# Softmax factors made beside an expert's second layer, from a copy of their logits

## The chip, the core and the metric

The kernel runs on one core of a Trainium2 chip. The metric is device time in microseconds (us) of one execution, as the median of several. A core has a matrix engine (PE, whose weight loads are listed as PEld), a vector engine (DVE), an activation engine (ACT), GpSimd (POOL) and a queue engine (SP) that here issues most of the DMAs. Each engine runs its own instructions strictly in their order, and an instruction that waits holds up all that stand behind it.

## What is computed

A recurrent attention is followed by a mixture of eight experts and a second pair of layers. The part that matters here is the mixture:

```python
logits = x @ w_gate
e_idx = np.argmax(logits, axis=1)
probs = np.exp(logits - logits.max(-1, keepdims=True))
probs /= probs.sum(-1, keepdims=True) + 1e-09
gate_w = probs[np.arange(N), e_idx]
eom = 1.0 / (1.0 + np.exp(-(x @ w_output_gate)))
for e in range(E):
    mask = e_idx == e
    h = np.maximum(x[mask] @ w1[e], 0.0)
    out[mask] = gate_w[mask, None] * eom[mask, e, None] * (h @ w2[e])
```

Then comes `relu(out @ w_in)**2 @ w_out`. The factor `gate_w * eom` of a row is not needed before the very last layer: there its square multiplies the row of the result. It is called the factor below.

## The kernel before

The program has three parts one after the other: the attention with the routing of the rows (about 560 us), the eight experts (about 270 us) and the second pair of layers (about 370 us). The change lies in the part of the experts.

**An expert** (e0 to e7) has 448 rows in a dense pass. Its first layer makes eight blocks of hidden values, f0 to f7, each with eight matmuls into a PSUM tile `ph` (line 1185). There are three such tiles, so block f4 can only start when block f1 has been read out of its tile. It is read by ACT (`hw`, line 1253, the high part) and then by DVE (`hw`, line 1254, the low part); both read `ph`. After blocks f5, f6 and f7 the PE also makes four transposes each (line 1226) for the next expert's rows `x`. The second layer is 64 matmuls (line 1356) in three groups: 16, 24 and 24. A group ends with a read by ACT (`yT`) and a DMA to `yTD` on SP (line 1365).

**The weights** of the next expert come in pieces (the generator `pieces`): SP loads a piece into one of four slots of `raws` (line 909), ACT makes its rounded high part (line 922) and POOL subtracts to get the low part (line 923), which frees the slot for the next load. The ACT instruction for a piece stands after each of the blocks f0 to f5, and there are two more in the second layer.

**Beside the second layer** the function `beside(e, s, nxt)` is called with s = 0, 1, 2, 3, before the matmuls 0, 16, 32 and 48. With s = 0 it loads the rows of the expert after next (`load_x`, line 1237). With s = 0, 1 and 2 it makes a step of `wide`, which turns a block of 64-bit weights into 32-bit ones: an ACT instruction (line 1151), five on DVE (lines 1152 to 1155 and 1167), one on POOL (line 1156) and a load of a later block on SP (line 1141). With s = 3 it issues the first four loads of the weights of the expert after next on SP.

**The factors** come from `gates`, a generator of three steps that is run in the first layer, one step after each of the blocks f0, f1 and f2. The first step has two small DVE instructions (lines 987 and 988), the second two on ACT (exponentials, lines 990 and 991), and the third six on DVE (lines 993 to 999) on tiles of 128 x 4 values, one of which reads 128 x 32. After the last block, ahead of the second layer, two DMAs on SP (line 1342) write the tile `gt` to `gtD` in DRAM, at a place that is only known at run time. Both write the same DRAM tensor at such places, and SP waits for the first to land before it issues the second. At the turn to the second pair SP loads all of `gtD` into `GT` (line 1383), and a DVE instruction `TID` (line 1384) reads it ahead of the pair's other DVE work.

All instructions of this part stand in an order written out by hand, which is the order of the code, engine by engine. At its very end, around the turn to the second pair, some of them are interleaved with those of the next part.

Of the kernel before, what the change touches and what calls it, by code (L numbers as in the profile page):

```python
# [7 lines left out]
F32 = mybir.dt.float32  # L8
# [4 lines left out]
AF = mybir.ActivationFunctionType  # L13
# [5 lines left out]
B, H, S, D = 4, 8, 768, 40  # L19
T = 32  # tokens of a chunk  # L20
NCH = S // T
WIN = 12  # chunks between two rescalings of the state
W_LO, W_HI = 0.84, 1.13  # decays that the scaled form covers
RSC = 2.0**24  # centres W_LO^(T WIN) .. W_HI^(T WIN) in the range of the square root
E = 8
ARENA = 12288  # words of a partition: the weights of an expert in two parts
F1 = 1024
F2 = 2048
CAP = 448  # rows of an expert that the dense pass covers
RS = 3200  # rows reserved per expert  # L30
NOV = 24  # blocks of 128 rows beyond CAP, at most
NP = 104  # partitions of the (head of pair at 0 / 64, feature) layout
# [5 lines left out]
XW = 402  # a routed row: 320 values, the last 64 again, 16 logits, number of the token (twice)  # L38
Y0 = 128  # the first of the tokens by expert, without gaps
YR = Y0 + S * B + CAP  # with room for the padding of the last expert  # L40
# [30 lines left out]
def layout(r, k, v, w, a, b, moe_w_gate, moe_w_output_gate, moe_w1, moe_w2, moe2_w_in, moe2_w_out):  # L71
# [7 lines left out]
    def tr(x):  # chunk, head of pair, feature, (pair, batch), token  # L79
        return x.reshape(B, 4, 2, NCH, T, D).transpose(3, 2, 5, 1, 0, 4).reshape(NCH, 2, D, 16, T)  # L80

# [13 lines left out]
    def rows(z):  # 320 rows as 128 + 128 + 64 twice  # L95
        z = np.concatenate([z, z[..., 256:320, :]], axis=-2)
        z = z.reshape(z.shape[:-2] + (3, 128, z.shape[-1]))
        return np.moveaxis(z, -3, -2)
# [14 lines left out]
ORDER = [  # stage, chunk relative to the iteration, argument  # L113
# [38 lines left out]
TAIL = [  # the last two iterations: stage, chunk relative to the last one, argument  # L152
# [73 lines left out]
HEAD = [  # the stages before the first regular iteration: stage, chunk, argument  # L226
# [70 lines left out]
EARLY = [2, 3, 5, 0]  # the first chunks for which DVE does a share of GpSimd's work  # L297


def attention(ctx, tc, nc, A, K, R, nch=NCH, order=ORDER, head=HEAD, tail=TAIL):  # L300
# [20 lines left out]
    def early(shape):  # L321
        """part of the arena: the buffers here are done with some chunks before the end"""
# [74 lines left out]
    # ---- loads  # L397
# [33 lines left out]
    # ---- decays: W (before a token) and C (after it), scaled a, b, k  # L431
# [20 lines left out]
    def A_rec2(c):  # L452
        # third-order step: 1 / C = y (t^2 - 3 t + 3), t = C y
# [27 lines left out]
    # ---- a.b and a.k of all pairs of tokens of a chunk  # L481
# [56 lines left out]
    # ---- inverse of the unit triangular system: 16 x 16 blocks, then the pair  # L538
# [65 lines left out]
    # ---- state  # L604
# [82 lines left out]
    # ---- outputs  # L687
# [72 lines left out]
    # ---- routing  # L760
# [49 lines left out]
def program(tc, A, out, nch=NCH, order=ORDER):  # L810
    nc = tc.nc
    V, G, S_, P = nc.vector, nc.gpsimd, nc.scalar, nc.tensor
    with ExitStack() as top:
# [31 lines left out]
        # ---- routing of 128 tokens  # L845
# [28 lines left out]
        def beyond():  # L874
            """whether there are rows beyond CAP, or decays out of range, or too few of the rows that are read ahead"""
# [22 lines left out]
        W1E = [732 * i for i in range(7)] + [5120, 5632]  # pieces of an expert's weights, the last 64 columns of the second ones apart  # L898
        W2I = [768 * i for i in range(9)]

        def pieces(slot, src, at, slots=4):
            """weights as the sum of two float32r parts, piece by piece"""
# [11 lines left out]
            for i in range(len(at) - 1):  # L914
                rw = ahead.pop(i)
                if at[i + 1] == 5632:  # high and low parts side by side
# [17 lines left out]
        def first_piece():  # L934
            if not first_w:
                first_w.extend([pieces(0, A["we"][0], W1E, 3)])
            elif not ring:  # in the place of the arena
                ring.append(cp.tile([128, ARENA], F32, name="ring0", tag="arena"))
            drain(first_w[0], 1)

        def zero(k):
            """rows of zeros: no row of xsD is read before it is written"""
# [8 lines left out]
        def rows_ahead():  # L951
            """rows that expert 0 most likely has already, without its last chunks"""
# [6 lines left out]
        def flag(pm):  # L959
            """whether a decay was out of range"""  # L960
# [19 lines left out]
        def gates(pool, x, g, e):  # L980
            """g: token (0) and the square of its factor (1) for the rows x (logits in 384:400) of expert e, step by step;
            relu(g a)^2 = g^2 relu(a)^2 as g >= 0"""
            a8 = list(x.shape[:-1]) + [8]
            L, O = x[..., 384:392], x[..., 392 + e]
# [8 lines left out]
            V.tensor_copy(g[..., 0], x[..., 400])  # L993
# [7 lines left out]
        def places():  # L1001
            """where the rows of an expert start in ysD"""
# [3 lines left out]
        def blocks(pool):  # L1006
            """the last blocks of 128 rows of an expert, beyond CAP"""
            V.tensor_scalar(out=pv, in0=pv, scalar1=0.0, scalar2=None, op0=ALU.max)
            # the first 512 rows are read before the dense pass of the last expert: if it has a part of them,
            # all its rows count as beyond CAP, and come before those of the other experts  # L1010
# [20 lines left out]
        with ExitStack() as ctx:  # L1031
# [5 lines left out]
            with tc.If(other > 0):  # L1037

                # ---- general path for decays out of range: token by token
# [40 lines left out]
                # ---- rows beyond CAP  # L1080
                blocks(op)
                for e in [E - 1] + list(range(E - 1)):
# [3 lines left out]
                    with tc.For_i(0, n_e, 1) as i:  # L1086
# [7 lines left out]
                        drain(gates(op, xo, go, e))  # L1094
# [31 lines left out]
        # ---- expert layers  # L1126
# [6 lines left out]
        def widths(src, n, step, ready):  # L1133
            """float64 weights, as pairs of words, to float32 (rounded to nearest), step by step"""
# [8 lines left out]
            def front(o):  # L1143
                """c: bits of |w|, the high word's 20 of the mantissa, then plus the low word's rounded"""
# [27 lines left out]
        def split_x(pk, x3, k, c):  # L1172
            """x3: [128, 5, n]: hi0 lo0 hi1 lo1 (hi2; lo2)"""
# [34 lines left out]
        def load_y(i):  # L1208
            """512 columns of the second layer pair's input, in the order of the experts"""
# [18 lines left out]
        with ExitStack() as ctx:  # L1228
# [22 lines left out]
            def hidden(ph, t, c):  # L1251
                """columns c of the hidden values: high parts, low parts"""
# [219 lines left out]
```

## Time and profile before

| | |
|---|---|
| Time, median of three executions | 1192.63 us (1191.32 to 1192.74) |
| Profiled execution: its time from first to last instruction (span) | 1201.3 us |
| of which attention and routing, experts, second pair | 560, 270.4, 370.9 us |
| Busy in the span: PE, PEld, DVE, ACT, POOL | 86%, 76%, 69%, 54%, 40% |
| Granted clock of PE over the span | 0.876 of full speed |

The profile comes from one execution that was recorded, and it is 8.7 us longer than the median of those that were only timed. No time other than the span is given for it. Stretches and durations are read from it; a difference of two stretches is carried over to the median as it is.

### The profile page before, as it was taken

Reading aid. Unit: us, or ns where it says so; the run is one execution under the profiler, and the core shown is the slowest. Engines: PE = TensorE matmul, PEld = TensorE weight load, DVE = VectorE, ACT = ScalarE, POOL = GpSimd, SP = SyncE. Lnnn points to the kernel's source line nnn. Section 1 sums busy time; section 2 is a strip of 40 time slices with the busy share of each in tenths; the row PEclk is TensorE's granted clock in tenths of the full one; section 3 lists DMA queues with packets and bytes.
Section 4 is the critical chain, followed back from the end, with each engine's and each line's share of the span. In section 5 each row is a group of like instructions: output and inputs, shape, how many; then the busy total and the mean of one; then the engine's idle time right before and its main releaser. Section 6 shows DMA issues by size and latency. Waiting matters only on the chain.

```text
span 1201.3 us, 31764 instructions
## 1 busy us (share of the span) xinstructions
PE 1038.2 (86%) x13114; PEld 911.5 (76%) x13114; DVE 829.3 (69%) x1827; ACT 652.6 (54%) x1407; POOL 476.9 (40%) x465
## 2 busy tenths in 40 slices
PE   2688888888897778887988889998989999999997
PEld 2577777777786666767877778886879998998986
DVE  6999998989989999653675566536993434344442
ACT  6587786776686776672444434334443343443432
POOL 6556464554554645341455455435541010101011
PEclk9977785869576886787989899999999999999999
DMA  5843333333332332243576667535330000000000
GB/s 139 265 124 83 87 93 86 98 83 92 86 92 72 104 86 70 82 122 125 133 200 168 179 188 187 146 115 131 104 97 23 27 23 27 23 1 23 2 21 22
DMA packets 56236, 114.99 MB, mean 96 GB/s; under 512 B 14608, under 2 KB 30096, under 8 KB 54160
## 3 DMA queue, kind: packets, MB, share of 16 engines
q1 hardware_dynamic: 50656, 100.47, 30.9%
q0 software_dynamic: 2688, 8.88, 1.9%
q10 hardware_dynamic: 2736, 3.49, 0.9%
q8 instruction: 106, 1.74, 0.6%
q14 instruction: 50, 0.41, 0.1%
HBM read 89.39 MB, written 23.43 MB: 94 GB/s over the span
## 4 chain that ended last, share of the span: by engine, by line
PE 31%; DVE 12%; DMA 6%; ACT 2%; issue 1%; SPq 1%; POOL 0%; POOLq 0%; ACTq 0%; DVEq 0%
PE ph L1185 17%; PE po L1189 4%; PE po L1190 4%; PE po L1188 4%; DMA raws<-in_we_dram 2%; PE py L1356 2%; DMA q<-in_wi_dram 2%; DVE c L1153 1%; DVE hl L1408 1%; DVE q L1405 1%; DVE c L1167 1%; DVE gm L996 1%; DVE gt L997 1%; DVE gt L999 1%; DVE c L1154 1%
## 5 line engine op out<-in xcount | busy, mean ns | idle before, releaser
L1185 PE MATMUL ph<-x,ring 128*128 128x512 f32 (+2 forms) x1344 | 319.7, 387 | 27.2 <-DVE hw L1254 27.2
L1185 PEld LDWEIGHTS ph<-x,ring 128*128 128x128 f32 x1344 | 249.5, 197 | 63.0 <-DVE hw L1254 30.0
L923 POOL TENSOR_TENSOR ring<-raws,ring 128x732 fp32r<-128x732 f32 (+2 forms) x72 | 124.1, 1744 | 137.2 <-ACT ring L922 108.3
L1405 DVE TENSOR_TENSOR q<-r 128x512 f32<-128x512 f32 x96 | 73.0, 761 | 106.8 <-ACT r L1404 106.8
L1423 POOL DMA_INDIRECT out_dram<-o,TID x24 | 28.2, 1175 | 269.6 <-ACT o L1421 226.7
L1189 PE MATMUL po<-ring,hl 128*128 128x320 f32 x368 | 115.6, 314 | 7.3 <-DVE hl L1408 7.3
L1188 PE MATMUL po<-ring,hh 128*128 128x320 f32 x368 | 114.6, 311 | 2.8 <-ACT hh L1407 2.8
L474 POOL TENSOR_TENSOR arena<-arena 40x1024 f32<-40x1024 f32 x43 | 108.5, 2523 | 20.2 <-ACT arena L456 16.0
L1404 ACT ACTIVATE r<-ph 128x512 f32<-128x512 f32 x96 | 57.1, 595 | 108.6 <-PE ph L1185 108.6
L1190 PE MATMUL po<-ring,hh 128*128 128x320 f32 x368 | 114.2, 310 | 0.0
L1408 DVE TENSOR_TENSOR hl<-q,hh 128x512 fp32r<-128x512 f32 x92 | 72.5, 788 | 54.8 <-ACT hh L1407 54.8
L1407 ACT ACTIVATE hh<-q 128x512 fp32r<-128x512 f32 x92 | 58.2, 633 | 88.0 <-DVE q L1405 88.0
L1356 PE MATMUL py<-hw,ring 128*128 128x448 f32 x512 | 105.4, 365 | 0.0
L1356 PEld LDWEIGHTS py<-hw,ring 128*128 128x128 f32 x512 | 95.5, 188 | 7.6
L1254 DVE SCALAR_TENSOR_TENSOR hw<-ph,hw 128x448 fp32r<-128x448 f32 (+2 forms) x72 | 39.7, 567 | 88.2 <-ACT hw L1253 88.1
L1189 PEld LDWEIGHTS po<-ring,hl 128*128 128x128 f32 x368 | 69.6, 189 | 14.9 <-DVE hl L1408 11.1
L1188 PEld LDWEIGHTS po<-ring,hh 128*128 128x128 f32 x368 | 69.8, 190 | 7.5 <-ACT hh L1407 3.2
L450 POOL TENSOR_TENSOR arena<-Cx,arena 104x512 f32<-104x512 f32 x22 | 26.3, 1197 | 123.6 <-ACT xs L862 115.7
L1190 PEld LDWEIGHTS po<-ring,hh 128*128 128x128 f32 x368 | 69.7, 189 | 0.0
L922 ACT ACTIVATE ring<-raws 128x732 fp32r<-128x732 f32 (+2 forms) x72 | 56.9, 792 | 22.8 <-DMA raws<-in_we_dram 20.5
L1253 ACT ACTIVATE hw<-ph 128x448 fp32r<-128x448 f32 (+2 forms) x72 | 35.8, 498 | 57.8 <-PE ph L1185 57.6
L439 DVE TENSOR_TENSOR_SCAN Cx<-arena 104x528 f32<-104x528 f32 x24 | 61.0, 2540 | 7.0 <-DMA arena<-in_xE_dram 6.3
(215 smaller groups left out, 2257.7 us busy)
## 6 DMA issues: line engine op xcount, KB each, us to landing
raws<-in_we_dram SPq DMA_DIRECT2D x48, 366.0 KB
arena<-in_xE_dram SPq DMA_DIRECT2D x48, 322.5 KB
xL<-in_xL_dram SPq DMA_DIRECT2D x24, 480.0 KB
xsD<-raws SPq DMA_DIRECT2D x24, 268.0 KB
q<-in_wi_dram SPq DMA_DIRECT2D x16, 384.0 KB
xg<-xsD SPq DMA_DIRECT2D x7, 804.0 KB
q<-in_wo_dram SPq DMA_DIRECT2D x16, 320.0 KB
wb<-in_wB_dram SPq DMA_DIRECT2D x24, 165.0 KB
```

The source lines that it names most:

```text
L439: V.tensor_tensor_scan(out=Cx.rearrange("p a b->p (a b)"), data0=s["w"], data1=d1[0:NP].rearrange("p a b->p (a b)"), initial=0.0, op0=ALU. ...
L474: (V if c < EARLY[2 + hh] else G).tensor_tensor(out=bd[sl, :, :, hh].rearrange("p a b c x->p (a b) c x"), in0=s["bk"][sl].rearrange("p (a ...
L923: G.tensor_tensor(out=lo, in0=rw, in1=hi.bitcast(F32), op=ALU.subtract)
L1185: P.matmul(ps, t[:, o : o + 128], x3[:, i, c], start=(j == 0), stop=(j == 7))
L1188: P.matmul(ps, hh, whi[:, o : o + 320], start=start, stop=False)
L1189: P.matmul(ps, hl, whi[:, o : o + 320], start=False, stop=False)
L1190: P.matmul(ps, hh, wlo[:, o : o + 320], start=False, stop=stop)
L1356: P.matmul(py, w, x, start=(f == 0 and k == 0), stop=last)
L1404: S_.activation(r, ph, AF.Relu)
L1405: V.tensor_tensor(out=q, in0=r, in1=r, op=ALU.mult)
L1407: S_.activation(hh, q, AF.Copy)
L1408: V.tensor_tensor(out=hl, in0=q, in1=hh.bitcast(F32), op=ALU.subtract)
```

## The change

`gates` is no longer drained in the first layer. At the start of an expert's first layer one ACT instruction copies the 18 columns of the logits and the token number of each row into a new tile `gl` (line 1333 of the new kernel). A new generator `factors` runs `gates` on that copy and ends with the two DMAs to `gtD` (line 1307 of the new kernel). `beside` runs one step of it with s = 0, 1 and 2, ahead of its other work. `gates` now takes columns 0 to 17 instead of 384 to 401; the rare path for rows beyond the dense pass passes it the columns accordingly. Comments were also taken out.

```diff
-            L, O = x[..., 384:392], x[..., 392 + e]
+            L, O = x[..., 0:8], x[..., 8 + e]
...
-            V.tensor_copy(g[..., 0], x[..., 400])
+            V.tensor_copy(g[..., 0], x[..., 16])
...
-                def beside(e, s, nxt):
+                def factors(e, off):
+
+                    gt = ep.tile([128, 4, 2], F32, name="gt", bufs=2)
+                    gl = glog.pop(e)
+                    yield from gates(ep, gl, gt, e)
+                    why = "the experts have at most S * B rows together"
+                    for j, n in ((0, 384), (3, 64)):
+                        p = min(n, 128)
+                        at = nc.s_assert_within(off + 128 * j, 0, YR - n, skip_runtime_bounds_check_because=why)
+                        nc.sync.dma_start(out=gtD[bass.ds(at, n)].rearrange("(j p) x->p j x", p=p), in_=gt[0:p, j : j + n // p])
+
+                def beside(e, s, nxt, gate):
+                    if s < 3:
+                        drain(gate, 1)
                     if s < 2 + (e == 0):
                         drain(nxt[2], 1)
...
-                    gt = ep.tile([128, 4, 2], F32, name="gt", bufs=2)
-                    gate = gates(ep, xg[e], gt, e)
+                    gl = glog[e] = ep.tile([128, 4, 18], F32, name="gl", bufs=2)
+                    S_.activation(gl, xg[e][:, :, 384:XW], AF.Copy)
...
-                        drain(gate, 1)
...
+                    gate = factors(e, off)
                     why = "the experts have at most S * B rows together"
-                    for j, n in ((0, 384), (3, 64)):
-                        p = min(n, 128)
-                        at = nc.s_assert_within(off + 128 * j, 0, YR - n, skip_runtime_bounds_check_because=why)
-                        nc.sync.dma_start(out=gtD[bass.ds(at, n)].rearrange("(j p) x->p j x", p=p), in_=gt[0:p, j : j + n // p])
...
-                            beside(e, i // 16, nxt)
+                            beside(e, i // 16, nxt, gate)
```

On DVE, this is the first layer of e3 in the kernel before: the low parts `hw` of the blocks, and between those of the third and the fourth block the six instructions of the last step of `gates`.

```order
L1254 SCALAR_TENSOR_TENSOR hw<-ph,hw 128x448
L987 TENSOR_REDUCE gm<-xg 128x4
L988 TENSOR_TENSOR gd<-xg,gm 128x32
L1254 SCALAR_TENSOR_TENSOR hw<-ph,hw 128x448 x2
L993 COPY gt<-xg 128x4
L995 TENSOR_REDUCE gm<-gd 128x4
L996 TENSOR_SCALAR gm<-gm 128x4
L997 SCALAR_TENSOR_TENSOR gt<-gt,gm 128x4
L998 RECIPROCAL gt<-gt 128x4
L999 TENSOR_TENSOR gt<-gt 128x4
L1254 SCALAR_TENSOR_TENSOR hw<-ph,hw 128x448 x3
```

After the change the last three groups of DVE in the second layer of e2 are these: the six instructions of e2's factors, a step of `wide` (`c` and `q` are its tiles), and then e3's first layer.

```order
L993 COPY gt<-gl 128x4
L995 TENSOR_REDUCE gm<-gd 128x4
L996 TENSOR_SCALAR gm<-gm 128x4
L997 SCALAR_TENSOR_TENSOR gt<-gt,gm 128x4
L998 RECIPROCAL gt<-gt 128x4
L999 TENSOR_TENSOR gt<-gt 128x4
L1152 TENSOR_SCALAR c_13003<-q_12938 128x384
L1153 TENSOR_SCALAR c_13003<-c_13003 128x384
L1154 TENSOR_SCALAR c_13003<-c_13003 128x384
L1155 TENSOR_SCALAR c_13003<-c_13003 128x384
L1167 SCALAR_TENSOR_TENSOR c_12966<-q_12728,c_12966 128x384
L1254 SCALAR_TENSOR_TENSOR hw<-ph,hw 128x448 x6
```

So six low parts of e3 now follow each other with nothing between them, and the six small instructions stand ahead of the step of `wide` with s = 2.

On SP, this is what stands in the second layer of e2 before: the end of the two DMAs to `gtD`, the rows of e4, the loads `q` of `wide`, two results `yTD`, and the first four weight loads for e4.

```order
L1342 DMA gtD<-gt 64x2
L1237 DMA xg<-xsD 128x4x402
L1141 DMA q_12942<-in_wi_dram 128x768
L1365 ISA
L1365 DMA yTD<-yT 64x448
L1141 DMA q_12977<-in_wi_dram 128x768
L1141 DMA q_13006<-in_wi_dram 128x768
L1365 REGISTER_ALU
L1365 DMA yTD<-yT 128x448
L909 DMA raws<-in_we_dram 128x732 x4
```

And this is the same place after the change.

```order
L1237 DMA xg<-xsD 128x4x402
L1141 DMA q_12938<-in_wi_dram 128x768
L1375 ISA
L1375 DMA yTD<-yT 64x448
L1141 DMA q_12975<-in_wi_dram 128x768
L1307 ISA
L1307 DMA gtD<-gt 128x3x2
L1307 ISA
L1307 DMA gtD<-gt 64x2
L1141 DMA q_13012<-in_wi_dram 128x768
L1375 REGISTER_ALU
L1375 DMA yTD<-yT 128x448
```

The row that follows is again that of the four weight loads. The two DMAs to `gtD` now stand between the second and the third load `q`, so the third `q`, a result and the four weight loads queue behind them.

## Rows read from the trace of the kernel before

**Rows 1.** Busy time per stretch: the first layers of e1 to e7.

```profile
core 0: us, PE busy (x) PEld busy (x) DVE busy (x) ACT busy (x) POOL busy (x), PEclk, DMA share, GB/s
596.74:619.54 22.80, 18.30 (x78) 15.60 (x76) 15.07 (x24) 10.38 (x20) 12.69 (x8) 0.85 0.66 194
632.46:653.70 21.24, 16.87 (x77) 14.32 (x75) 11.01 (x17) 9.95 (x19) 10.32 (x6) 0.92 0.64 175
666.85:689.50 22.65, 18.06 (x77) 15.31 (x76) 11.71 (x17) 9.96 (x19) 10.30 (x6) 0.85 0.63 168
702.42:724.40 21.98, 17.58 (x77) 14.82 (x75) 11.54 (x17) 10.07 (x19) 10.29 (x6) 0.84 0.67 171
737.57:758.08 20.51, 17.51 (x78) 15.16 (x76) 11.74 (x17) 10.30 (x19) 10.33 (x6) 0.83 0.64 152
771.00:789.71 18.71, 16.73 (x78) 14.40 (x76) 10.97 (x17) 10.13 (x19) 10.35 (x6) 0.91 0.45 135
802.85:817.63 14.78, 13.07 (x65) 11.92 (x64) 9.57 (x16) 9.90 (x18) 10.12 (x6) 1.00 0.74 250
```

**Rows 2.** The same view for the second layer of e2.

```profile
653.70:666.85 13.15, 13.15 (x66) 12.13 (x66) 10.32 (x18) 4.51 (x9) 6.94 (x5) 1.00 0.67 180
```

**Rows 3.** Timeline of DVE, first layers of e0 and e3: start, us, instruction.

```profile
576.62 0.16 DVE L997 SCALAR_TENSOR_TENSOR gt<-gt,gm 128x4 f32<-128x4 f32 x1
...
675.04 1.29 DVE L993 COPY gt<-xg 128x4 f32<-128x4 f32 x1
...
678.08 1.65 DVE L997 SCALAR_TENSOR_TENSOR gt<-gt,gm 128x4 f32<-128x4 f32 x1
...
681.36 1.67 DVE L1254 SCALAR_TENSOR_TENSOR hw<-ph,hw 128x448 fp32r<-128x448 f32 x3
```

**Rows 4.** Timeline of PE, first layers of e0 and e3; idle time in brackets.

```profile
578.77 1.89 PE L1185 MATMUL ph<-x,ring 128*128 128x256 f32 x8 [2.68 <-DVE hw L1254]
...
673.82 3.49 PE L1185 MATMUL ph<-x,ring 128*128 128x448 f32 x16 [0.41 <-DVE hw L1254]
677.15 0.69 PE L1226 MATMUL pk<-cst,xg 128*128 128x128 f32 x4
682.02 3.36 PE L1185 MATMUL ph<-x,ring 128*128 128x448 f32 x8 [4.18 <-DVE hw L1254]
```

**Rows 5.** Timeline of SP, first to sixth expert.

```profile
598.71 1.98 SPq L909 DMA_DIRECT2D raws<-in_we_dram  x4
...
662.43 3.06 SPq L1141 DMA_DIRECT2D q<-in_wi_dram  x2
...
666.19 2.27 SPq L909 DMA_DIRECT2D raws<-in_we_dram  x4
...
681.46 3.92 SPq L1342 DMA_DIRECT2D gtD<-gt  x2
...
735.13 1.85 SPq L909 DMA_DIRECT2D raws<-in_we_dram  x4
...
767.50 1.82 SPq L909 DMA_DIRECT2D raws<-in_we_dram  x4
```

**Rows 6.** Waits of SP, experts: line, waited for, us in total, times, longest.

```profile
SPq L1342 <- DMA gtD<-gt: 25.7, 8, 4.6
```

**Rows 7.** Timeline of DVE and POOL in the second layer of e2.

```profile
655.56 1.82 DVE L1153 TENSOR_SCALAR c<-c 128x384 f32<-128x384 f32 x1
...
661.80 0.55 DVE L1167 SCALAR_TENSOR_TENSOR c<-q,c 128x384 int32<-128x384 int32 x1
...
662.03 1.20 POOL L1156 TENSOR_TENSOR c<-c,r 128x384 int32<-128x384 int32 x1 [1.15 <-DVE c L1155]
...
664.55 0.55 DVE L1167 SCALAR_TENSOR_TENSOR c<-q,c 128x384 int32<-128x384 int32 x1
669.23 0.62 DVE L1254 SCALAR_TENSOR_TENSOR hw<-ph,hw 128x448 fp32r<-128x448 f32 x1 [4.12 <-ACT hw L1253]
```

**Rows 8.** The chain that ended last, around the second layer of e2.

```profile
666.19 5.66 DMA raws<-in_we_dram
671.87 0.82 ACT ring L922
```

**Rows 9.** Granted clock after an idle PE in e1's first layer.

```profile
605.20:610.10 4.90, 4.86 (x16) 4.35 (x17) 4.12 (x5) 3.35 (x9) 4.90 (x4) 0.65 0.88 270
```

**Rows 10.** Timeline at the turn to the second pair.

```profile
832.98 0.43 SPq L1383 DMA_DIRECT2D GT<-gtD  x1
...
837.50 0.18 DVE L1384 CAST TID<-GT 128x24 int32<-128x24 f32 x1 [4.93 <-DMA GT<-gtD]
```

More of the change, by code (lines that the diff above doesn't have):

```diff
@@ L1093, in program @@
                         go = op.tile([128, 1, 2], F32, name="go")
-                        drain(gates(op, xo, go, e))
+                        drain(gates(op, xo[..., 384:XW], go, e))
                         nc.sync.dma_start(out=w1t.rearrange("p a b->p (a b)"), in_=A["we"][e, :, 0 : 3 * F1])
@@ L1311, in beside @@
                         drain(wide, 1)
+                glog = {}
                 wide = work()
```

## The prediction

> **What bounds the kernel now.** I read the stretches first, then the timelines of PE, DVE and SP over two experts, then the waits and the chain. The change lies in the 270 us of the experts. Their second layers need no help: e2's takes 13.15 us for 64 matmuls, PE is busy throughout and the granted clock is 1.00 [rows 2]. That is 0.205 us for a matmul.
>
> The first layers of e1 to e6 have the same 64 matmuls and three groups of four transposes, 0.69 us each [rows 4], a little less where they overlap. At the same rate that is 13.1 + 1.9 = 15.0 us, but they take 18.71 to 22.80 us [rows 1]. e7 has no transposes: 14.78 us against 13.1. So the excess is 7.8, 6.2, 7.6, 7.0, 5.5 and 3.7 us for e1 to e6 and 1.7 us for e7. e0 adds the 2.7 us that its PE sat idle [rows 4]. The sum is **42.2 us**.
>
> In e3 the excess has two causes. The large one comes after block f5: PE sits idle for 4.18 us until a DVE `hw` frees a tile `ph` [rows 4]. DVE began its group of six small factor instructions at 675.04 and only came back to `hw` at 681.36 [rows 3]. Six instructions on four values per partition took 6.3 us. The same instruction, line 997, took 0.16 us in e0 and 1.65 us in e3 [rows 3], where POOL worked without a pause: six instructions, 10.30 us busy in e3's first layer [rows 1]. So most of the six instructions wait for the end of a POOL instruction. The second part is the clock: the eight matmuls after that pause took 3.36 us instead of 1.64 [rows 4], which is the lower level of 1.2 GHz.
>
> The smaller cause is a pause of 0.41 us before f4 [rows 4]. It ends the chain from the weight loads: issued at 666.19, landed 5.66 us later, then an ACT piece ahead of the `hw` of f1 [rows 8]. PE could start f4 at 673.82, 7.6 us after that issue. This second chain is just behind the first layer's own pace, and it is what the change touches with its other hand.
>
> **What is removed.** All eight experts lose the six instructions between the `hw` of their first layer, two small ones before, and two on ACT. I take it that without them the whole excess of 42.2 us would be open to be saved, except what the weight loads hold back. A copy of 128 x 72 values is added on ACT, at the start of the first layer where ACT waits for PE anyway. It is smaller than any ACT instruction on a weight piece, 0.82 us [rows 8]; I take nothing, and at most 8 x 0.8 = 6 us if nothing hid it.
>
> **What is moved on DVE.** In e2's second layer DVE is busy for 10.32 of 13.15 us [rows 2] and stands still from 665.1 to 669.23 [rows 7], so two or three more us there delay no `hw`. Without that gap they would cost 2 us an expert. But POOL works in this layer too, and the small instructions wait for it again: line 1153 took 1.82 us there [rows 7]. The two of the first step stand ahead of that one and take over most of its wait; I add 0.6 us. The six then follow the `wide` instruction that ends at 661.80 + 0.55 = 662.35, or 8.65 us after the layer's start. A POOL instruction runs from 662.03 to 663.23 just then [rows 7]. Lower bound for the six: 6 x 0.16 = 1.0 us; upper bound: 6.3 us as in the first layer [rows 3]. With one POOL instruction in the way I take 2.0 us. So the factors are ready 8.65 + 0.6 + 2.0 = 11.3 us after the layer's start.
>
> **What is moved on SP.** This is where the price is. Before, the two DMAs to `gtD` stood at the end of the first layer, where SP had nothing urgent. The second waits for the first to land: 25.7 us over eight experts, 3.2 us each and at most 4.6 [rows 6]. With both issues the pair takes 3.92 us in e3 [rows 5] and, from the mean wait and two issues of half a us, about 4.3 us on average. After the change, queued behind the pair are a load for `wide`, a result, and the four weight loads, which take part in the second chain above.
>
> Before, these loads were issued 666.19 - 653.70 = 12.5 us after e2's second layer began [rows 1, 5], and e1 and e3 are alike. After: 11.3 + 4.3 + 0.8 for the two issues ahead of them = 16.4 us, so **3.9 us later**. f4 can start 7.6 us after that, at 24.0 us. PE gets there at 13.15 + 6.6 = 19.7 us. The pause before f4 is then 24.0 - 19.7 = 4.3 us. The clock also falls again after such a pause: in e1 PE now pauses in that very place and the 16 matmuls behind it ran at a granted 0.65, 4.86 us instead of 3.3 [rows 9]. I add 1.7 us for each pause over 2 us.
>
> The Trainium skill speaks to the pair: its page "DMA: Bandwidth & Descriptors", section "Anatomy of one DMA", puts a fixed cost of about 2.0 us on a small DMA, most of it the confirmation that the write has landed. The trace differs, with 3.2 us [rows 6], and the trace's number is the one in the sum. With 2.0 us the pause would be 1.2 us shorter in five experts, and the saving 6 us larger.
>
> **The sum.** First layers after the change, excess over 15.0 us: e1 to e4 4 x (4.3 + 1.7) = 24.0 us. I treat e1 like the others: its loads were issued at 598.71 [rows 5], late already, but its `wide` loads will no longer stand behind the pair of e0. e5: its loads were issued 10.7 us after the layer's start [rows 1, 5] and go to 16.0, as one issue less is ahead of them: pause 3.9, with the clock 5.6 us. e6: 9.4 us before [rows 1, 5]; no `wide` load is left there and the factors are ready some 2.5 us earlier, so 13.6, and a pause of 1.5 us. e7 and e0: nothing. Together 24.0 + 5.6 + 1.5 = 31.1 us. Saved: 42.2 - 31.1 = 11.1 us.
>
> At the turn, `GT` is now loaded behind e7's pair and has to wait until its second DMA has landed. Before it was issued at 832.98, 15.4 us after e7's second layer began, and `TID` held DVE until 837.50 [rows 1, 10]. After: e7's factors wait for POOL and for a step of the 64-bit weights between them, so I put the pair at 12 us and its end at 17 or 18. I take off **2 us** (bounds 0 and 5). That leaves **9 us**, and 1192.6 - 9 = 1183.6, given as 1183.
>
> **The rivals.**
> *The loads are not late enough to matter.* If the factors are ready at 10 us and the pair takes 3.2 us, the loads are 1.5 us late and most pauses stay under 2 us with no loss of clock. Then excess stays about 2 us in each of e1 to e5 and some 30 us are saved: 1163 us. For it: DVE is not full in the second layer [rows 2], and the six could slip into a gap with no POOL instruction beside them. Against it: the wait of 3.2 us is a mean over eight [rows 6], and a POOL instruction does run where the six begin [rows 7].
> *Slower: the pair takes longer in its new place.* A `wide` load is issued right ahead of it, and another and the rows of the expert after next shortly before. If the pair lands only behind these, each exposed layer loses the difference. Five are exposed, so 9 us are gone at 1.8 us more, a pair of 6.1 us; at 8 us it would be 1192.6 + 9.5 = 1202. Against it: the pair stood right behind weight loads before, too, and its longest wait was 4.6 us [rows 6].
> On the Trainium skill's page "DMA: Bandwidth & Descriptors", section "Queues, rings and completion order", a completion signal lands only after all earlier writes of its DMA engine, which would be this mechanism; no row here shows whether it is at work.
> *No change:* the pause moves from f6 to f4 and is as long there, 1192 us. The excess after and before would be equal; this is the forecast with 2 us more of wait per expert.
>
> **How the numbers follow.** A measurement of this kernel can tell some 0.2%, 2.4 us, from no change. Forecast (2.4 to 20 us saved): 0.50. Loads hardly late: 0.20. No change: 0.12. Slower: 0.18. So faster 0.70. The range must reach to the gain of the first rival, 1163, and to the slower one near its break-even, 1195: the pair at 6.5 us, or the turn at its upper bound with the pair at 6. About one in ten lies beyond each end.
>
> **What the new profile would show.** Right: no small DVE instruction between the `hw` of a first layer, and the pause of PE gone from f6. `gtD` issued near 11 us into the second layer, weight loads near 16, and a pause of some 4 us before f4 at half the clock behind it. Wrong: weight loads still near 12.5 us (the large gain), or a pair of over 6 us (slower), or a `TID` that comes much later than 20 us after e7's second layer began.

## The result and the profile after

The change makes the kernel **slower**: 1211.24 us, median of four executions (1201.04 to 1213.08), against 1191.97 us (1191.28 to 1192.74) of the kernel before. The ratio is 1.0148, with a 95% interval of 1.0102 to 1.0195. Ratios, here and below, leave out executions more than 1.5% above the fastest of the same kernel and are not the quotients of the medians beside them; the two differ by up to 0.35%. The prediction said 1183 us, with 0.18 for slower.

The profiled execution has a span of 1210.5 us, a granted clock of 0.867 over it and 1212.32 us in the times. Busy shares are PE 87%, PEld 76%, DVE 66%, ACT 54%, POOL 39%. Since single executions of one kernel differ by some 10 us, both kernels were run again later, unchanged. In the stretch from the first matmul of e0 to the first matmul `po` of the second pair the two traces of each give this (starts and ends from the timeline of PE and the windows):

| us | before | before, again | after | after, again | forecast of the change | measured, means |
|---|---|---|---|---|---|---|
| e0 | 36.2 | 36.3 | 32.4 | 32.1 | -2.7 | -4.0 |
| e1 to e6 | 206.1 | 198.8 | 207.2 | 210.1 | -6.7 | +6.2 |
| e7 | 27.6 | 27.6 | 36.2 | 33.3 | -1.7 | +7.1 |
| the turn, up to `po` | 8.6 | 6.8 | 11.6 | 11.8 | +2 | +4.0 |
| sum | 278.5 | 269.5 | 287.3 | 287.3 | -9.1 | +13.3 |

Ahead of e0 and behind `po` the traces of the two kernels show no loss (behind `po` 362.3 us before and 362.0 after, in the first two). So the loss lies where the change does. Between the medians it is 19.3 us, and 17.0 us when both were run again; the 4 to 6 us that these traces do not locate are within the spread of single executions. Busy time by stretch in the profiled execution after the change: the first layers of e1 to e6, then e7's first layer, its second, and the turn.

```profile
core 0: us, PE busy (x) PEld busy (x) DVE busy (x) ACT busy (x) POOL busy (x), PEclk, DMA share, GB/s
593.59:617.30 23.71, 17.45 (x78) 15.09 (x76) 7.45 (x14) 10.21 (x19) 11.67 (x8) 0.86 0.78 213
630.21:652.26 22.05, 16.91 (x77) 14.48 (x75) 5.54 (x9) 10.03 (x18) 11.02 (x7) 0.92 0.70 197
665.40:686.39 20.99, 16.78 (x78) 14.49 (x76) 5.53 (x9) 10.01 (x18) 10.83 (x7) 0.92 0.72 208
699.31:720.65 21.34, 16.82 (x78) 14.40 (x76) 5.54 (x9) 10.13 (x18) 11.03 (x7) 0.92 0.71 206
733.79:754.67 20.88, 16.79 (x77) 14.52 (x75) 5.53 (x9) 10.05 (x18) 11.16 (x7) 0.92 0.70 190
767.59:787.60 20.01, 16.92 (x77) 14.47 (x75) 5.53 (x9) 10.00 (x18) 10.35 (x6) 0.91 0.66 167
800.75:814.58 13.83, 13.08 (x66) 11.92 (x64) 3.12 (x5) 6.02 (x11) 7.26 (x4) 1.00 0.80 201
814.58:836.91 22.33, 17.22 (x66) 14.07 (x64) 15.86 (x29) 8.95 (x18) 12.17 (x8) 0.77 0.41 129
836.91:848.47 11.56, 7.66 (x26) 5.32 (x24) 1.45 (x5) 2.57 (x6) 0.86 (x1) 0.78 0.38 64
```

Beside [rows 1], DVE has lost half its work in the first layers (e3: 11.71 to 5.53 us), as the change says. The layers of e1 to e6 are no shorter for it, 129.0 us together against 127.9 in [rows 1], and e7's second layer takes 22.33 us instead of 12.8 before.

The timeline of DVE, and below it that of POOL, in e2's second layer, which began at 652.26:

```profile
653.73 0.18 DVE L987 TENSOR_REDUCE gm<-gl 128x4 f32<-128x32 f32 x1
653.95 1.60 DVE L988 TENSOR_TENSOR gd<-gl,gm 128x32 f32<-128x32 f32 x1
...
661.12 0.98 DVE L993 COPY gt<-gl 128x4 f32<-128x4 f32 x1
...
662.91 0.16 DVE L999 TENSOR_TENSOR gt<-gt 128x4 f32<-128x4 f32 x1
...
653.75 1.75 POOL L923 TENSOR_TENSOR ring<-raws,ring 128x728 fp32r<-128x728 f32 x1 [2.38 <-ACT ring L922]
...
660.88 1.20 POOL L1156 TENSOR_TENSOR c<-c,r 128x384 int32<-128x384 int32 x1 [1.15 <-DVE c L1155]
```

The six instructions cost 2.0 us, as forecast: only the first has a POOL instruction in its way. The factors are ready 10.8 us after the layer's start (forecast 11.3). The timelines of SP and PE, from e2's second layer on, show what follows in e3:

```profile
663.10 3.65 SPq L1307 DMA_DIRECT2D gtD<-gt  x2
...
668.64 2.23 SPq L909 DMA_DIRECT2D raws<-in_we_dram  x4
...
676.18 5.04 PE L1185 MATMUL ph<-x,ring 128*128 128x448 f32 x16 [4.21 <-DVE hw L1254]
```

The weight loads are issued 16.4 us after the layer's start, and f4 starts 7.5 us behind them, after a pause of 4.21 us. Both times are the forecast to a tenth. The 16 matmuls behind the pause take 5.04 us instead of 3.3, at a granted clock of 0.65 from 676.18 to 681.06. The pause in the middle of f5 to f7 [rows 4] is gone. SP's waits in the experts, beside [rows 6]:

```profile
SPq L1307 <- DMA gtD<-gt: 26.3, 8, 3.7
```

So the pair of DMAs did not get longer. With both issues it takes 4.4 us on average for e0 to e6, 4.3 forecast.

In e7 something else is seen. The timelines of SP and, in the last row, of ACT, from the end of e6 on:

```profile
799.70 1.83 SPq L909 DMA_DIRECT2D raws<-wiD  x4
801.77 1.82 SPq L1375 DMA_DIRECT2D yTD<-yT  x1
809.60 0.38 SPq L1213 DMA_DIRECT2D xg<-yTD  x1
...
811.92 2.69 SPq L909 DMA_DIRECT2D raws<-wiD  x4
...
816.26 0.85 ACT L922 ACTIVATE ring<-raws 128x768 fp32r<-128x768 f32 x1 [5.40 <-DMA raws<-wiD]
```

Early in e7 SP loads the results of the experts back from `yTD` (line 1213) for the second pair. This load waits until e6's last result has landed. e7's own second four weight loads stand behind it. They are issued 11.2 us after e7's start; in the trace of before, whose e7 starts at 802.85 [rows 1], it was 6.8 us (at 809.60 of that trace). ACT waits 5.40 us for them, and the `hw` of the last blocks stand behind that ACT instruction, so the second layer stalls. The wait for the result in SP's waits, first after the change, then before it:

```profile
SPq L1213 <- DMA yTD<-yT: 6.0, 1, 6.0
```

```profile
SPq L1213 <- DMA yTD<-yT: 3.1, 1, 3.1
```

After the change the result is issued 0.2 us behind the four weight loads (801.77, and 799.70 + 1.83), and the issue itself takes SP 1.82 us. Before, it stood 2.6 us behind them (803.67, and 799.25 + 1.83) and its issue took 0.34 us. The timeline of SP before:

```profile
799.25 1.83 SPq L909 DMA_DIRECT2D raws<-wiD  x4
803.67 0.34 SPq L1365 DMA_DIRECT2D yTD<-yT  x1
807.29 0.39 SPq L1213 DMA_DIRECT2D xg<-yTD  x1
...
809.60 4.05 SPq L909 DMA_DIRECT2D raws<-wiD  x4
```

The chain of waits at the turn:

```profile
832.85 0.08 DVE gt L999
832.95 5.64 DMA gtD<-gt
...
838.71 4.88 DMA gtD<-gt
...
843.61 3.32 DMA GT<-gtD
...
846.95 0.07 DVE TID L1394
```

e7's factors are ready at 832.93, 18.35 us into its second layer, not 12. Then three DMAs follow one another, 14 us in all, and `TID` comes at 846.95 instead of the 837.50 of [rows 10].

### The profile page after: what moved, and what is told of

It reads as the page before. It is cut to its first block, busy times and chain, and to the rows that moved or that the text cites. A ratio compares the mean times of both kernels' runs of the same rounds, so it can differ in the third digit from the quotient of the medians.

```text
span 1210.5 us, 31791 instructions
## 1 busy us (share of the span) xinstructions
PE 1048.5 (87%) x13114; PEld 920.1 (76%) x13114; DVE 800.8 (66%) x1827; ACT 652.1 (54%) x1415; POOL 477.4 (39%) x465
## 4 chain that ended last, share of the span: by engine, by line
PE 36%; DVE 7%; DMA 7%; issue 2%; ACT 1%; SPq 1%; POOLq 0%; POOL 0%; DVEq 0%; ACTq 0%
PE ph L1185 19%; PE py L1366 5%; PE po L1189 4%; PE po L1190 4%; PE po L1188 4%; DMA raws<-in_we_dram 3%; DMA gtD<-gt 2%; DVE hl L1418 1%; DVE q L1415 1%; PE pk L1226 1%; DMA raws<-wiD 1%; DMA out_dram<-o,TID 1%; DVE c L1167 1%; DVE c L1153 1%; ACT hw L1253 1%
## 5 line engine op out<-in xcount | busy, mean ns | idle before, releaser
L1185 PE MATMUL ph<-x,ring 128*128 128x512 f32 (+2 forms) x1344 | 319.2, 387 | 31.7 <-DVE hw L1254 28.1
L1185 PEld LDWEIGHTS ph<-x,ring 128*128 128x128 f32 x1344 | 248.9, 196 | 68.0 <-DVE hw L1254 30.7
L1366 PE MATMUL py<-hw,ring 128*128 128x448 f32 x512 | 109.8, 373 | 5.1 <-DVE hw L1254 3.5
L1156 POOL TENSOR_TENSOR c<-c,r 128x384 int32<-128x384 int32 (+1 forms) x32 | 34.8, 1088 | 58.3 <-DVE c L1155 42.0
```

Source lines behind the costliest of these rows:

```text
L1185: P.matmul(ps, t[:, o : o + 128], x3[:, i, c], start=(j == 0), stop=(j == 7))
L1366: P.matmul(py, w, x, start=(f == 0 and k == 0), stop=last)
```

## The experiments

The prediction's own mechanism is called Q here: the weight loads queue behind the pair on SP, and the wait of the pair's second DMA for the first eats what the first layers gain. The rivals at the start were T, that the loss is the turn behind e7, and plain variation between executions. Three more came up from traces: Y, that e7 is stretched by its weight loads behind the load from `yTD`; M, that ACT waits at the turn until the DMAs have read `gt`, because its next tile takes over that memory; and G, that the turn waits for `GT`. Ratios are to the kernel before, run beside each group on the same chip: one chip for `b2`, `e7_first`, `one_dma` and `pair_late`, a second for the others. A trace shows one execution; those of `b2`, `one_dma`, `pair_late`, `before_one`, `one_e7` and `after_y` are the fastest of their group, so they show where the time goes, and the ratios how much it is.

**The kernels unchanged** (`b2` is before, `after2` is after).

> The kernel before, unchanged, for a second trace of it: the profiled execution that the prediction was made from was 9 us longer than the timed ones, and the changed kernel is 19 us slower by the timed ones but only 9 us by the two profiles. Theory Q (the pair of DMAs to gtD on SP delays the weight loads) and theory T (the turn after e7) both expect 1192 us and first layers of e1 to e6 of 19 to 23 us as in the first trace. If the first trace was an unlucky one, the span here is about 1190 us and some first layers are shorter than there by 9 to 10 us in all; the sum of the prediction then began from an excess that was 10 us too large.

> The changed kernel, unchanged, beside the kernel before on this chip. Executions of one kernel were seen 5 to 13 us apart here, and its attention part alone took 549 to 560 us. Theory Q+T (both the loads behind the pair and the turn cost) expects the part of the experts, from e0's first matmul to the first matmul of po, at 285 to 290 us against 270 to 279 of the kernel before, and the time 12 to 20 us above it.

Measured: before 1191.81 us, ratio 1.0017 [0.9987, 1.0047]; after 1206.39 us, 1.0119 [1.0077, 1.0161]. The slowdown is there again, with before unchanged. From the first layers of e1 to e6 in the second trace of before:

```profile
758.57:775.74 17.17, 15.18 (x77) 13.24 (x75) 10.89 (x17) 10.06 (x19) 10.36 (x6) 1.00 0.48 148
sum 120.65, PE 100.63 PEld 86.63 DVE 71.05 ACT 60.90 POOL 64.39; mean PE 16.77 PEld 14.44 DVE 11.84 ACT 10.15 POOL 10.73
```

Their sum is 120.65 us, against 127.9 in [rows 1]: an excess over 6 x 15.0 us of 30.7, not 37.9. The execution on which the prediction rested had 7 us more to save than this one, which is the fastest of its ten. The second trace of after has 131.9 us there, the first 129.0.

**One DMA instead of the pair** (`one_dma` in the kernel after, `before_one` in the kernel before). The DMA writes all 512 rows of `gt`; the next expert overwrites the 64 that are too many.

```diff
-        gtD = dp.tile([YR, 2], F32, name="gtD")
+        gtD = dp.tile([YR + 64, 2], F32, name="gtD")
...
-                    for j, n in ((0, 384), (3, 64)):
-                        p = min(n, 128)
-                        at = nc.s_assert_within(off + 128 * j, 0, YR - n, skip_runtime_bounds_check_because=why)
-                        nc.sync.dma_start(out=gtD[bass.ds(at, n)].rearrange("(j p) x->p j x", p=p), in_=gt[0:p, j : j + n // p])
+                    at = nc.s_assert_within(off, 0, YR - CAP, skip_runtime_bounds_check_because=why)
+                    nc.sync.dma_start(out=gtD[bass.ds(at, 512)].rearrange("(j p) x->p j x", p=128), in_=gt)
```

> The changed kernel, with the factors written by one DMA of 512 rows in place of two of 384 and 64, so SP has no landing to wait for; the 64 rows too many are overwritten by the next expert's. Theory Q: the weight loads of e0 to e5 are issued 3.5 to 4 us earlier, 12.5 us after the second layer's start; the pause before f4 falls from 4 to 6 us to at most 1.5, the clock stays up, and the first layers of e1 to e6 take 15.5 to 18 us instead of 20 to 24: some 25 us less, about 1185 us. Theory T: those layers keep their length and only the turn gains the 5.8 us of e7's pair: about 1205 us.

> The kernel before, with the factors written by one DMA of 512 rows in place of two, and nothing else changed. Theory Q (the pair's wait only costs where weight loads are queued behind it): within 2 us of the kernel before, as behind the pair there stands only a load of rows that is needed an expert later. If two DMAs cost wherever they stand, it gains as much as one DMA did in the changed kernel, some 25 us or more.

Measured: `one_dma` 1170.88 us, ratio **0.9871** [0.9836, 0.9906]; `before_one` 1187.39 us, 0.9966 [0.9934, 0.9997]. SP in e3's second layer (it began at 660.70) and the first layers of e1 and e3 in `one_dma`:

```profile
671.55 0.41 SPq L1305 DMA_DIRECT2D gtD<-gt  x1
...
674.55 2.84 SPq L909 DMA_DIRECT2D raws<-in_we_dram  x4
```

```profile
582.46:599.14 16.68, 15.22 (x77) 13.16 (x75) 7.23 (x14) 9.89 (x19) 11.01 (x8) 1.00 0.85 264
...
643.38:660.70 17.32, 15.22 (x78) 13.18 (x76) 5.32 (x9) 9.69 (x18) 10.13 (x7) 1.00 0.75 217
```

The single DMA is issued at the same place, 10.85 us into the layer. SP does not wait for it, the weight loads come at 13.85 us, the first layers of e1 to e6 are 3.7 to 7.0 us shorter and the clock in them is 1.00. Most of the loss at the end of the loop goes too: e7 takes 29.8 us and the turn 8.1. The time is 14 us below the 1185 us expected, which had left the end out. In the old place the same edit brings a third of a per cent by the ratio, where no weight load stood right behind the pair. Its one trace, of an execution 10 us below the median, has 261.7 us in the stretch, 8 to 17 less than the two of before, so the traces do not settle how little the wait cost there. For the new place it is Q: the wait of the second DMA costs what stands behind it on SP. It turns a gain of 1.3% into a loss of 1.2 to 1.5%.

**e7's factors as before** (`e7_first`): only e0 to e6 are made beside the second layer.

```diff
                     yield from gates(ep, gl, gt, e)
+                    yield
...
-                        drain(gate, 1)
+                        drain(gate, 1 + (s == 2))
...
+                    gate = factors(e, off)
...
+                        if e == E - 1 and f < 3:
+                            drain(gate, 1)
...
-                    gate = factors(e, off)
+                    if e == E - 1:
+                        drain(gate)
```

> The changed kernel, but e7's factors and its two DMAs to gtD are made as before, in and behind its first layer; e0 to e6 stay beside the second layer. Theory T (the loss is at the turn: e7's pair is issued so late that GT, and everything that waits for gt to be read, comes some 9 us later): the PE's first matmul of po comes 8 to 10 us earlier, and the time is about 1200 us. Theory Q alone (the loss is in e0 to e6, where the weight loads queue behind the pair): the turn gains 2 us at most, about 1209 us.

Measured: 1199.09 us, ratio 1.0051 [1.0015, 1.0086]. e7's layers and the turn:

```profile
797.93:816.22 18.29, 14.68 (x65) 13.19 (x64) 9.20 (x15) 9.26 (x19) 9.81 (x6) 0.91 0.74 225
816.22:829.48 13.26, 13.08 (x65) 11.92 (x64) 11.85 (x20) 5.99 (x12) 7.77 (x6) 1.00 0.46 113
829.48:836.14 6.66, 5.75 (x26) 4.34 (x24) 1.77 (x6) 2.57 (x6) 1.86 (x2) 1.00 0.63 113
```

The turn is back to 6.66 us and e7 takes 31.6 instead of 33.3 to 36.2. So the end of the loop is the larger part of the net loss (T), but not all of it. Of what is left e7 has 4.0 us, and e0 to e6 have 2.2: 240.9 us, against 242.3 and 235.1 in the two traces of before. That `one_dma` brings most of the end back without this edit shows that the pair's wait stands behind both parts.

**The pair behind the weight loads** (`pair_late`).

```diff
                     yield from gates(ep, gl, gt, e)
+                    yield
...
                         later[0] = next_w(e + 2)
+                    if s == 3:
+                        drain(gate)
```

> The changed kernel, with the pair of DMAs to gtD issued behind the first four weight loads of the step s = 3 instead of ahead of them. Theory Q: first layers of e1 to e6 as with one DMA, 15.5 to 18 us, so 25 to 30 us less there; the turn gets later, since e7's pair is now the last thing ahead of GT: some 5 us lost. About 1190 us. Theory T: nothing gained in the layers and 5 us lost at the turn, about 1216 us.

Measured: 1195.78 us, ratio 1.0079 [1.005, 1.0109], little better than the change. The timelines of SP and, in the last row, of ACT, from the end of e0's second layer into e1; then the two layers of e1, by windows:

```profile
584.55 1.97 SPq L909 DMA_DIRECT2D raws<-in_we_dram  x4
586.71 7.32 SPq L1308 DMA_DIRECT2D gtD<-gt  x2
...
596.55 2.11 SPq L909 DMA_DIRECT2D raws<-in_we_dram  x4
...
602.14 0.81 ACT L922 ACTIVATE ring<-raws 128x732 fp32r<-128x732 f32 x1 [7.87 <-DMA raws<-in_we_dram]
```

```profile
584.13:599.94 15.81, 15.22 (x78) 13.17 (x76) 5.04 (x10) 6.23 (x12) 8.28 (x6) 1.00 0.70 183
599.94:617.70 17.76, 15.63 (x65) 12.95 (x65) 13.12 (x29) 8.31 (x17) 8.98 (x6) 0.90 0.63 213
```

The first layer falls to 15.8 us. But the first DMA of the pair now goes out 0.2 us behind four weight loads of 366 KB, the pair takes 7.3 us, and the *next* four loads come late. Part of the loss moves to the second layer: over e1 to e6 the first layers are 27.7 us shorter than after the change and the second layers 12.3 us longer. e7 and the turn stay at 35.2 and 12.2 us. SP's waits for the pairs of e0 to e6 in `pair_late`:

```profile
SPq L1308 <- DMA gtD<-gt: 43.3, 7, 6.6
```

That is 6.2 us a pair, nearly twice the 3.3 us of its place ahead of the loads.

**Both edits** (`one_e7`: the one DMA and e7's factors in its first layer).

> One DMA of 512 rows, and e7's factors made in its first layer as before; e0 to e6 beside their second layers. Theory Q+T: the first layers of e1 to e6 keep the 15 to 18 us of one DMA, and e7 with the turn, 37.9 us there from e7's first matmul to the first of po, takes 33 to 36 us as in the kernel before. So 2 to 4 us below one DMA, 1167 to 1169 us, and some 20 us below the kernel before. If the turn costs nothing once there is one DMA, it equals one DMA.

Measured: 1166.42 us, ratio **0.9773** [0.9716, 0.9829]. The stretch is 249.1 us, and pauses of 1.5 to 2.6 us before f4, with no loss of clock, are the main part of what is left in e1 to e5. How much e7's edit adds to the one DMA is not settled: the ratios differ by a per cent, but from groups on two chips; the medians are 22.9 and 18.7 us below the kernel before; and in the traces e7 and the turn take 36.0 us against 38.0 of `one_dma`, the whole stretch 0.8 us less.

**`gt` in memory of its own** (`gt_apart`, in the kernel after).

```diff
-                    gt = ep.tile([128, 4, 2], F32, name="gt", bufs=2)
+                    gt = mp.tile([128, 4, 2], F32, name="gt", bufs=2)
```

> The changed kernel, with the tile gt in a pool that stays open through the second pair, so no tile of the pair lies where gt was. Theory M (ACT's first read of the pair waits until e7's pair of DMAs has read gt, since its tile takes gt's memory; 6.1 us there): that wait is gone, PE's pause of 3.6 us ahead of its third block too, and 3 to 4 us are gained if nothing else is late. Theory G (GT is what the turn waits for; DVE waits 12.3 us for it): the waits of ACT and PE go, but the first matmul of po comes as late as before, and at most 1 us is gained.

Measured: 1204.72 us, ratio 1.0109 [1.0069, 1.015], the same as `after2`. After the change ACT's first read of the second pair waited 6.1 us for the pair's DMA to read `gt`:

```profile
843.75 0.60 ACT L1414 ACTIVATE r<-ph 128x512 f32<-128x512 f32 x1 [6.10 <-DMA gtD<-gt]
```

With `gt` apart this wait is gone, and `po` is no earlier (timelines of ACT, DVE and PE):

```profile
830.50 0.60 ACT L1414 ACTIVATE r<-ph 128x512 f32<-128x512 f32 x1 [1.32 <-PE ph L1185]
...
838.63 0.18 DVE L1394 CAST TID<-GT 128x24 int32<-128x24 f32 x1 [11.14 <-DMA GT<-gtD]
...
840.12 0.63 PE L1188 MATMUL po<-ring,hh 128*128 128x320 f32 x1 [5.92 <-ACT hh L1417]
```

ACT is 8 us ahead of `TID`, and the turn takes 11.7 us as it did. M falls; what holds the turn is `GT` (G).

**The load from `yTD` behind e7's weight loads** (`after_y`): it is issued with block f4 instead of at e7's start, and the split of its rows goes beside the second layer.

```diff
+                        if s:
+                            split_y(E, s - 1)
...
-                    if e == E - 1:
-                        load_y(E)
...
+                        if e == E - 1 and f == 4:
+                            load_y(E)
...
-                            else:
-                                split_y(E, f - 5)
```

> The changed kernel, but the load of the second pair's input from yTD is issued on SP behind e7's four weight loads instead of ahead of them, and its three splits by ACT and DVE are made beside e7's second layer. Theory Y (e7 is stretched because those weight loads wait on SP for a result of e6 to land in yTD, and ACT waits for the weights ahead of the last blocks of e7): the loads are issued 2 to 4 us earlier, the pauses in e7's second layer shrink, and e7's two layers take 27 to 30 us instead of the 33 to 36 of the changed kernel: 4 to 7 us less. Against it, theory T alone (only the pair and GT cost at the end): e7 keeps its 33 to 36 us.

Measured: 1201.56 us, ratio 1.0131 [1.0082, 1.0179]. e7's layers and the turn:

```profile
790.05:802.89 12.84, 12.84 (x65) 11.93 (x64) 3.75 (x6) 7.58 (x14) 7.58 (x5) 1.00 0.75 210
802.89:815.70 12.81, 12.81 (x66) 12.00 (x64) 5.89 (x13) 6.72 (x14) 7.00 (x4) 1.00 0.65 197
815.70:832.96 17.26, 9.75 (x25) 6.30 (x23) 7.60 (x21) 3.59 (x9) 4.57 (x5) 0.76 0.33 66
```

e7 takes 25.65 us, its least, with no pause at all: Y is shown for the place (the edit moves the load and its split together). The turn waits for `GT` behind the pair all the same and takes 17.26 us, so e7 and the turn together take 42.9 us against 47.7 and 45.1 after the change. The ratio does not tell it from `after2`.

**The last step moved too** (`one_late`: in `one_e7`, the third step and the DMA go behind the weight loads; `one_late_y`: with the edit of `after_y` besides).

```diff
-                    if s < 3:
-                        drain(gate, 1 + (s == 2))
+                    if s < 2:
+                        drain(gate, 1)
...
                         later[0] = next_w(e + 2)
+                    if s == 3:
+                        drain(gate)
```

> One DMA and e7's factors in its first layer, and for e0 to e6 the last step of the factors, with the DMA, stands beside the second layer behind the weight loads of s = 3. Theory Q: nothing of the factors is ahead of the weight loads any more, neither on SP nor, by the load q that waits for DVE, on DVE; they are issued 1 to 2 us earlier than with one DMA in s = 2, and the pauses of 1.5 to 2.6 us before f4 in e1 to e5 fall under 1: 5 to 9 us less than that kernel, 1158 to 1162 us. If those pauses come from the landing of the loads alone, no change, 1166 us.

> As the last one, and the load from yTD behind e7's weight loads with its splits beside e7's second layer. Theory Y: e7's two layers, 28.7 us with one DMA and e7 as before, take 26.5 to 27.5 us: 1 to 2 us less than the last one. If the load is then late for the second pair, the turn loses as much.

Measured: `one_late` **1160.21 us** (1159.51 to 1162.58), ratio 0.9775 [0.9741, 0.9809]; `one_late_y` 1165.2 us, 0.9798 [0.974, 0.9856]. e1's first layer in `one_late`, by windows:

```profile
586.84:601.77 14.93, 14.93 (x77) 13.24 (x75) 5.64 (x12) 8.63 (x16) 9.74 (x6) 1.00 0.97 285
```

e1 reaches the 15.0 us that the prediction took for a first layer without excess; the stretch is 240.5 us. `one_late` is the best kernel here, some 27 us faster than before. The ratios do not tell it from `one_e7`, though the stretches of their traces do by 8.6 us. The edit to the load from `yTD` brings nothing more, and Y's expectation failed here: e7 took 31.7 us, not 26.5 to 27.5. With the weights there early, its first layer took 18.88 us against 14.78 in `one_late`. PE waited 3.06 us for a `hw` behind e7's last step of the factors, which DVE made from 768.14 to 774.26, with single instructions of up to 1.75 us.

## Why the prediction was wrong

**Right: what happens in a first layer.** Each step measured close to its number: factors ready at 10.8 us (11.3), pair 4.4 us (4.3), weight loads at 16.4 (16.4), f4 7.5 us behind them (7.6), a pause of 4 to 5 us in e2 to e5 and a lower clock behind it. `one_dma` shows that the pair's wait is the cost. The small DVE instructions are gone from there, and with the wait gone the forecast's first rival, 1163 us, comes about in kind: 1171 us with one DMA, an excess of 0.1 to 3.2 us a layer, and 1160 to 1166 with the further edits.

**Wrong, the step that failed: "e7 and e0: nothing".** e7 was to save 1.7 us and costs 7.1: 8.8 us of the 22.4 between the forecast of -9.1 us and the +13.3 measured in the stretch. The mechanism was missed here: a term was put at nothing without a reason. The largest part of the distance, 12.9 us, is one of size in e1 to e6, below. With e7 put right alone the sum would have been no change (-0.3 us), with e1 to e6 alone a loss of 3.8 us. The prediction counted what is queued on SP behind the pair in e1 to e6, and did not follow the same queue into e7. There a load waits for e6's last result to land. After the change the weight loads issued in e6 come 2.6 us later against e7's start and the result right behind them; its landing is waited for twice as long, and the weight loads of e7 stand behind. That the `yTD` load ahead of the weights stretches e7 is shown by `after_y`, where it moves together with the split of its rows. The split is no cause by itself: it stood in e7 before, too, when e7 took 27.6 us.

What makes the result land late was not tried by itself. In the four traces with the result 0.2 to 0.4 us behind the loads the wait is 5.8 to 6.0 us; in the six with 2.6 us it is 2.9 to 3.5 (`before`, `b2`, `before_one`) but 4.4 to 5.4 in `one_dma`, `one_e7` and `one_late`. Counted from the end of the weight loads' issue, the result had landed after 6.0 to 8.5 us in all ten. Of the 4.4 us by which e7's loads are issued later, 2.6 are those of the loads in e6; why the way from them to the landing is longer as well stays open.

**Wrong in size, and the largest part: the excess of e1 to e6**, forecast to fall from 37.8 to 31.1. By means over two traces it went from 34.3 to 40.5, 12.9 us from the forecast. Of this 3.5 us were hardly there to be saved: the prediction took the excess from one execution, 8.7 us longer than the median, and carried it over as it was. The other 9.4 us are the 31.1 that came out too small, by e1 (8.7 and 8.6 us instead of 6.0), e6 (5.0 and 6.3 instead of 1.5), e5 (5.9 and 7.8 instead of 5.6) and e2 to e4 (1.3 together). In e6 the loads came at 14.5 us, not 13.6, and f4 8.3 us behind them; the pause was 3.1 us and the clock fell as well. In e1 "like the others" did not hold: the four issues took 4.4 us, the fourth alone 2.95 us without a wait that the trace shows, and f4 came 9.4 us behind the first. The bound of 2 us, over which a pause was to cost clock, has no row behind it: in [rows 9] the clock fell after a pause of 1.93 us, and in `one_e7` pauses of up to 2.63 us were followed by 16 matmuls in 3.5 us.

**Wrong in size: the turn**, 4.0 us instead of 2, within its bounds of 0 to 5. The end of the pair was put at 18 us into e7's second layer; it came at 29, as the layer itself was stretched and each of the three DMAs took 3.3 to 5.6 us. A `TID` "much later than 20 us" was named as a sign of a wrong prediction; it came at 32.4.

**e0** gave 4.0 us instead of 2.7. With the three others: 8.8 + 12.9 + 2.0 - 1.3 = 22.4 us.

**The rivals.** The slower one was right in sign only. Its mechanism, a pair of over 6.1 us in its new place, held at most for e7's alone (6.3 and 5.8 us with both issues in the two traces), where no weight load queues behind it, and in another place in `pair_late` (6.8 to 7.8 us). For e0 to e6 the pair was as short as before. For e1 to e6 by themselves "no change" came nearest: the pause moved from f6 to f4, and the excess is 37.9 and 39.0 us in the first two traces. Its reason, 2 us more of wait per expert, was not seen. The 2.4 us that a measurement was to tell rested on three executions; 25 later ones of the kernel before lie between 1181.6 and 1200.2 us.

## What to carry to other kernels

When work moves in a queue, follow the queue to the last iteration and through the turn behind it: the same delay met another load there, and 11 of the 13 us lost, net of what e0 gained, lie in the last expert and the turn. Before DMAs are moved ahead of something urgent, ask whether the issuing queue waits *inside* the moved group; one DMA of 512 rows instead of two turned the same change from 1.2% slower into 1.3% faster. And an excess that is read from one execution is worth no more in a sum than its spread between two: 37.9 and 30.7 us here.

## What the runs showed of the hardware

**Small DVE instructions and POOL.** Within one expert DVE's TENSOR_REDUCE (line 987) took 0.18 us while a POOL instruction ran, and the TENSOR_TENSOR behind it, with both inputs in SBUF, 1.60 us: it ended as POOL's did, and so did the COPY at 661.12. The last TENSOR_TENSOR of the group, with POOL idle, took 0.16. The Trainium skill's page "SBUF — State Buffer", section "Who interferes with whom", says that a DVE instruction with two SBUF inputs contends with a POOL instruction that reads SBUF, and that a reduction never does; the rows agree.

**How long SP waits for a DMA to land depends on what went ahead.** The first DMA of the pair, some 3 KB, was waited for 3.3 us on average ahead of the weight loads (26.3 us over eight) and 6.2 us right behind them (43.3 over seven). The result of e6 was waited for 5.8 to 6.0 us in the four traces where it stood 0.2 to 0.4 us behind weight loads, and 2.9 to 5.4 us in the six where it stood 2.6 us behind. Its issue took SP 1.3 to 1.9 us in the first four and 0.34 us in the others.

**One kernel's executions differ.** The start of e0 fell between 550 and 561 us in thirteen traces, though no edit touches the instructions ahead of it.
